# A fused attention and feed-forward kernel: the planner's order replaced by a written one, table loads as tasks of their own, separate banks for the first transposes, one silu for the last chunk

## The chip, the cores and the metric

The kernel runs on one core of a Trainium2 chip. A core has five instruction streams that matter here: PE (TensorE: matmuls and transposes, with the weight loads listed apart as PEld), DVE (VectorE), ACT (ScalarE), POOL (GpSimd) and SP (SyncE, which issues most DMAs). Each stream is carried out in its own order; they wait for one another through semaphores. Matmuls write to PSUM, which has eight banks of 128 partitions by 512 float32 numbers; ACT and DVE empty them.

The metric is the device time of one launch in microseconds (us). The profile is one execution, taken by the hardware profiler; its "span" leaves out what lies around the program.

## The reference

The input `x` has 2048 tokens of 448 numbers. It is normalised once, and the result feeds two branches whose outputs are multiplied:

```python
def _A_ref(x, wqkv, wo):            # H = 16 heads of Dh = 28, W = 8 keys, 2 apart
    qkv = (x @ wqkv).reshape(B, S, 3, H, Dh) ...
    idx = pos[:, None] - (arange(8) * 2)[None, :]
    logits = where(idx >= 0, q . k[idx] * Dh ** -0.5, -1e9)
    o = softmax(logits) . v[idx]
    return o.reshape(B, S, D) @ wo

def _B_ref(x, w1, b1, w2, b2):      # 448 -> 1792 -> 448
    return gelu_tanh(x @ w1 + b1) @ w2 + b2

xn = layernorm(x)
return x + _A_ref(xn, ...) * silu(_B_ref(xn, ...))
```

## The kernel before

**Tiling.** Tokens are split into even and odd ones, so that a dilation of 2 becomes neighbours. There are 16 token tiles of 128 (NT) in four chunks of 512 (NCH). The 448 features are three full row tiles of 128 and one of 64; the last one is held twice, so that two matmuls of 64 rows can run side by side in the array.

**Steps.** For each token tile: `stats` (DVE), `rstds` (ACT and DVE for tiles 0 to 3, POOL for the rest), `norm` (DVE), and a transposition of the normalised tile into `xnT`. Tiles 0 to 3 are transposed by PE into a PSUM bank and copied out by ACT or DVE; the rest go through a DMA transpose on SP. `qk_rows` and `vproj` (lines 532 and 556) make q, k and v; q and k are transposed by DMA into `qkT`, and rows of v are moved by POOL's DMAs into window buffers. For the first two tiles `first_batch` runs three full row tiles of q, k and v together, `kt` = 0, 1, 2, each needing its own third of `w_in`. All other projections and the first feed-forward layer `ff1` (line 591) are made in pairs (`pair`): four row-tile steps, a no-op on SP or POOL that waits for them, then three more steps. Each pair takes two banks, and its two results are emptied by ACT (gelu, line 595) or copied by ACT or DVE. `ff2` (line 627) takes seven gelu results at a time into one bank; then `y` = bank + b2 on DVE, tanh on ACT (line 655), and `g` = (tanh + 1) * y on DVE (line 659).

**Attention** goes in nine blocks. "S" (line 677): 64 small matmuls of 32 rows fill four banks with scores; ACT takes the exponentials (line 687) and DVE or POOL multiply by a mask (line 693). "P" (line 709): 64 matmuls of 64 rows and 32 columns sum the values into two banks; DVE then transposes, inverts, transposes back and multiplies into `oT` (lines 719 to 733). `final` (line 796) multiplies `oT` by `wo`; DVE makes `sg` = bank * 0.5 * g (line 801), `o` = x + sg (line 807), and SP stores it.

**What sets the order.** Every step is a task (`_Task`) with an engine, a cost, dependencies and the buffers that it takes and gives back. `_Plan.run` lets all engines go through the tasks in modelled time and picks by hand-set priorities (`PRIO`, `LATER`); `emit` writes the instructions in the order of the modelled start. An instruction waits only for what it needs, but nothing on its engine overtakes it. ACT needs another function table for square root, for gelu and for exp; a load stands in front of the first activation that needs it, and `tanh` is in the table of either of the latter two. Some 14 to 17 matmuls on a zeroed tile (`warm`, line 327) run at the start.

Of the kernel before, what the change touches and what calls it, by code (L numbers as in the profile page):

```python
# [13 lines left out]
HOP = 0.10  # L14
SLACK = 0.12
TABLE = 1.28
SWITCH = 0.095
TILED = 30
SAME = 20
HOPS = ("POOL", ("SP", "POOL"))  # L20
MASK_ON = (("DVE", "POOL"), (0.4, 1.2))


def VISITS(bs):
    out = [[("S", b)] for b in bs[:2]]
    for i, b in enumerate(bs):
        out.append([("P", b)] + [("S", c) for c in bs[i + 2:i + 3]])
    return out


class _Pool:


    def __init__(self, bufs, fifo=False):
        self.bufs = bufs
        self.fifo = [] if fifo else None
        self.free = [(0.0, i) for i in range(len(bufs))]


class _Task:  # L40
    __slots__ = ("eng", "cost", "deps", "fn", "prio", "take", "give", "slots",
                 "start", "end", "on", "ndep", "users", "tail", "seq", "table", "limit", "mode", "out")


class _Plan:

# [4 lines left out]
    def add(self, eng, cost, fn, deps=(), prio=0, take=(), give=(), tail=0.0, table=(), limit=None,  # L53
            mode=128):
        t = _Task()
        t.eng = eng if isinstance(eng, tuple) else (eng,)
        t.cost = cost if isinstance(cost, tuple) else (cost,) * len(t.eng)
        t.deps = [d for d in deps if d is not None]
        t.fn, t.prio, t.give, t.tail, t.table, t.limit = fn, prio, give, tail, table, limit
        t.mode, t.out = mode, None  # L60
        t.take = {}
        for p in take:
            t.take[p] = t.take.get(p, 0) + 1
        t.slots = {}
        t.start = t.end = None
        t.on = None
        t.users = []
        t.seq = len(self.tasks)
        self.tasks.append(t)
        for p in t.take:  # L70
            if p.fifo is not None:
                p.fifo.append(t)
        return t

    def _at(self, t, e, free):
        at = free.get(e, 0.0)
        for p, n in t.take.items():
            if len(p.free) < n or p.fifo and p.fifo[0] is not t:
                return None
            at = max(at, sorted(p.free)[n - 1][0] + HOP)  # L80
        if t.table and self.table not in t.table:
            at += TABLE
        for d in t.deps:
            at = max(at, d.end - d.tail if d.on == e else d.end + HOP)
        if e == "PE" and t.mode != self.mode:
            at = max(at, free.get(e, 0.0) + SWITCH)
        return at

    def run(self):
        for t in self.tasks:  # L90
            t.ndep = len(t.deps)
            for d in t.deps:
                d.users.append(t)
        free = {}
        self.table = None
        self.mode = 128
        ready = [t for t in self.tasks if not t.ndep]
        order = []
        while ready:
            cand = []  # L100
            for t in ready:
                ways = []
                for e, c in zip(t.eng, t.cost):
                    at = self._at(t, e, free)
                    if at is not None:
                        ways.append((at + (c if len(t.eng) > 1 else 0.0), at, e, c))
                if ways:
                    _, at, e, c = min(ways)
                    cand.append((at, t, e, c))
            if not cand:  # L110
                raise RuntimeError("the plan is stuck: " + str([(t.seq, t.eng, t.fn.__qualname__) for t in ready[:20]]))
            first = min(cand, key=lambda k: k[0])
            near = [k for k in cand if k[2] == first[2] and k[0] <= first[0] + SLACK]
            tiled = first[2] == "PE" and self.mode < 64
            at, t, e, c = min(near, key=lambda k: (-k[1].prio - (TILED if tiled and k[1].mode < 64 else SAME if k[2] == "PE" and k[1].mode == self.mode else 0),
                                                   k[0], k[1].seq))
            if t.limit is not None and at > t.limit:
                t.fn, c = None, 0.0
            t.on, t.start = e, at
            if e == "PE" and t.fn is not None:  # L120
                self.mode = t.out or t.mode
            if t.table and self.table not in t.table:
                self.table = t.table[0]
            free[e] = at + c
            t.end = at + c + t.tail
            for p, n in t.take.items():
                got = sorted(p.free)[:n]
                for g in got:
                    p.free.remove(g)
                t.slots[p] = [g[1] for g in got]  # L130
                if p.fifo is not None:
                    p.fifo.pop(0)
            for p, owner, i in t.give:
                p.free.append((t.end, owner.slots[p][i]))
            ready.remove(t)
            order.append(t)
            for u in t.users:
                u.ndep -= 1
                if not u.ndep:
                    ready.append(u)  # L140
        assert len(order) == len(self.tasks)
        self.order = sorted(order, key=lambda t: (t.start, t.seq))
        self.span = max(t.end for t in order)
        return self

    def emit(self):
        done = set()
        for t in self.order:
            for d in t.deps:
                assert id(d) in done  # L150
            done.add(id(t))
            if t.fn is not None:
                t.fn(t)

# [10 lines left out]
def kernel(  # L165
# [12 lines left out]
    nc = tc.nc  # L178
# [67 lines left out]
    def ring(name, n, shape, dt=BF16, fifo=False):  # L246
        return _Pool([sb(f"{name}{i}", shape, dt) for i in range(n)], fifo)
# [3 lines left out]
    p_E = ring("E", 8, [P, 512], fifo=True)  # L251
# [10 lines left out]
    p_h = ring("h", 28, [P, CH], fifo=True)  # L262
    p_v = ring("v", 6, [P, H, 32], fifo=True)
    qk_tok = [sb(f"qk_tok{i}", [P, 2, H, 32]) for i in range(4)]
    p_b = _Pool([psum.tile([P, 512], F32, name=f"bank{i}") for i in range(8)])

    p_tok = _Pool([None])


    PRIO = {  # L270
        "project": (49.5, 205, 104, 52.5,),
        "project2": (147, 150, 101, 61,),
        "values": (89.5, 62.5, 21, 58,),
        "attn": (185, 179.5, 78, 174.5, 106.5, 106, 138.5, 136.5, 32.5,),
        "ff1": (185, 180, 84.5, 176.5, 66.5, 64.5, 156.5, 189.5, 203, 146, 76, 114.5, 77.5, 179.5,
            75.5, 118.5, 180.5, 14.5, 163, 68, 151, 115.5, 194.5, 167.5, 180, 188.5, 86, 93,),
        "gelu": (62.5, 22.5, 95, 92.5,),
        "ff2": (144, 162.5, 103.5, 142.5, 44.5, 112.5, 67, 5, 89, 106.5, 101.5, 75, 74, 55, 11.5,
            6.5,),
        "final": (140, 19.5, 70.5, 47, 112, 34.5, 23.5, 142.5, 73, 53, 198.5, 188.5, 81.5, 126.5,  # L280
            180, 71,),
        "norm": (37.5, 132, 179.5, 129.5, 74.5, 99, 161, 69, 63, 62, 43.5, 73, -5.5, 90, 133.5,
            150,),
        "loads": (166.5, 166, 188, 139.5, 54.5,),
        "stats": (47.5, -60, 180.5, 23, 127, 56, 188.5, 77, 197.5, -13.5, 185, 205.5, 138, 14, 52.5,
            138.5,),
        "turn_x": (108.5, -1, 28, 116, 210, 116.5, 131.5, 160, 41.5, 79.5, 70, 119, -4.5, 74.5,
            132.5, 111,),
        "turn_qk": (68.5, 112, 174.5, 90, 80, 6, 149.5, 60.5, 4, 140.5, 199.5, 96.5, 103, 166.5,
            140, 156,),  # L290
        "move_v": (81.5, 95, 23, 95, 18.5, 26.5, 8, 128, 29.5,),
        "copies": (50, 119.5, 58.5, 76, 32.5, 135.5, 43, 1, 87, 79.5, 129, 77, 32, 41.5, 135,),
    }
    LATER = {"swap": 135, "qk": 165, "v": 29.5, "gelu": 30.5, "exp": 55.5, "mask": -60, "pv": 45, "recip": -16.5, "os": 54.5, "y": 153.5, "tanh": 182.5, "g": 58, "sg": 183, "o": 120.5}
# [5 lines left out]

    def pe(n, k=1):
        return k * (n / 2400.0 + 0.0025)

    def act(n):
        return 0.15 + n / 1130.0

    def dve(n, r=1):
        return 0.15 + n / (960.0 * r)
# [12 lines left out]

    warm = p_h.bufs[-1]
    t_on = plan.add("DMA", 0.8, lambda _: None, (), 100)
    t_warm = plan.add("DVE", 0.3, memset("vector", warm[:], 0.0), [t_on], prio=100)
    for i in range(48):
        def fn(k, n=512 if i < 9 else P):
            nc.tensor.matmul(buf(p_b, k)[:, :n], warm[:, :P], warm[:, :n], start=True, stop=True)  # L327
# [288 lines left out]
    def ff2_part(t, cs, n, end, prio):  # L616
# [26 lines left out]
        if t == NT - 1:  # L643
            prio += 9
# [322 lines left out]
```

## Time and profile before

| what | value |
|---|---|
| time, median of 3 runs | 157.99 us (157.61 to 159.14) |
| span of the profiled execution | 156.2 us |
| PE busy | 150.1 us |
| matmuls of the second layer (L627, 238) | 45.2 us |
| matmuls of the first layer (L591, 392) | 44.7 us |
| matmuls of q, k (L532, 212) and v (L556, 106) | 24.3 and 13.4 us |
| matmuls of the output (L796, 68) | 14.1 us |
| function table loads on ACT | 6, of 1.28 us each |
| DVE busy between 59 and 94 us | 31.4 of 35 us |

The page gives, for each group of instructions, the busy time, the mean duration, and the idle time of its engine before it with what ended it. Idle time of an engine costs something only if someone waits for that engine. The chain of waits is followed back from the last instruction, so it says what held the end back. A matmul's record is longer than the time that it holds the array up (a 448-column matmul is 0.35 us long, and the next starts 0.19 us after it), so PE's pace is read from starts.

### The profile page before, as it was taken

Reading aid. Unit: us, or ns where it says so; the run is one execution under the profiler, and the core shown is the slowest. Engines: PE = TensorE matmul, PEld = TensorE weight load, DVE = VectorE, ACT = ScalarE, POOL = GpSimd, SP = SyncE. Lnnn points to the kernel's source line nnn. Section 1 sums busy time; section 2 is a strip of 40 time slices with the busy share of each in tenths; the row PEclk is TensorE's granted clock in tenths of the full one; section 3 lists DMA queues with packets and bytes.
Section 4 is the critical chain, followed back from the end, with each engine's and each line's share of the span. In section 5 each row is a group of like instructions: output and inputs, shape, how many; then the busy total and the mean of one; then the engine's idle time right before and its main releaser. Section 6 shows DMA issues by size and latency. Waiting matters only on the chain.

```text
span 156.2 us, 5305 instructions
## 1 busy us (share of the span) xinstructions
PE 150.1 (96%) x2204; PEld 77.8 (50%) x2204; DVE 113.2 (72%) x259; ACT 83.3 (53%) x149; POOL 74.7 (48%) x123
## 2 busy tenths in 40 slices
PE   6999999999999999999999999999999999999980
PEld 2544454444455555455554644455556444545570
DVE  4789551486266758997799895109899996998992
ACT  3245867378889416444634149782496587051220
POOL 7854856000459408839261098389599780000000
PEclk9999999999999999999999999999999999999999
DMA  4999969999749443099039822123300100200211
GB/s 156 329 317 315 167 124 187 237 269 307 141 95 166 64 82 90 10 192 138 4 83 85 131 70 73 38 76 83 105 0 4 34 31 29 63 4 0 68 36 43
DMA packets 33575, 17.36 MB, mean 111 GB/s; under 512 B 25331, under 2 KB 32387, under 8 KB 33552
## 3 DMA queue, kind: packets, MB, share of 16 engines
q1 hardware_dynamic: 31472, 14.03, 41.3%
q0 software_dynamic: 1936, 2.88, 8.5%
q8 instruction: 17, 0.28, 0.8%
q10 hardware_dynamic: 144, 0.11, 0.2%
q14 instruction: 6, 0.05, 0.1%
HBM read 7.06 MB, written 1.84 MB: 57 GB/s over the span
## 4 chain that ended last, share of the span: by engine, by line
PE 80%; DVE 8%; DMA 3%; POOL 2%; issue 2%; ACT 1%; SPq 1%; DVEq 0%; ACTq 0%; POOLq 0%
PE bank L627 23%; PE bank L591 22%; PE bank L532 11%; PE bank L796 7%; PE bank L556 6%; PE bank L677 4%; PE bank L709 4%; PE bank L327 3%; DMA xnT<-xn 3%; POOL v L354 2%; DVE sg L801 2%; DVE o L807 1%; DVE w_in L659 1%; ACT E L687 1%; DVE xn L438 1%
## 5 line engine op out<-in xcount | busy, mean ns | idle before, releaser
L627 PE MATMUL bank<-w,h 128*128 128x448 bf16 (+1 forms) x238 | 45.2, 342 | 0.0
L591 PE MATMUL bank<-xnT,w 64*128 64x512 bf16 x392 | 44.7, 376 | 0.0
L595 ACT ACTIVATE h<-bank,b 128x512 bf16<-128x512 f32 x56 | 34.0, 689 | 12.9 <-PE bank L591 12.8
L354 POOL DMA_DIRECT2D v<-v_tok x52 | 27.6, 538 | 19.8 <-PE bank L709 9.0
L693 POOL TENSOR_TENSOR E<-E,m_gen 128x456 bf16<-128x456 bf16 x24 | 26.7, 1139 | 11.7 <-ACT E L687 9.5
L627 PEld LDWEIGHTS <-h 128*128 128x128 bf16 x238 | 22.3, 98 | 18.1 <-issue 0.4
L591 PEld LDWEIGHTS <-w 64*128 64x128 bf16 x392 | 19.1, 94 | 22.7 <-issue 1.1
L532 PE MATMUL bank<-w_in,xnT 64*128 64x448 bf16 (+1 forms) x212 | 24.3, 350 | 0.1
L687 ACT ACTIVATE E<-bank 128x456 bf16<-128x456 f32 (+1 forms) x36 | 17.0, 555 | 9.1 <-PE bank L677 9.1
L655 ACT ACTIVATE t<-y 128x448 f32<-128x448 f32 x15 | 8.7, 578 | 17.4 <-DVE y L649 17.4
L719 DVE STREAM_TRANSPOSE dt<-bank 128x480 f32<-128x480 f32 (+1 forms) x18 | 12.1, 671 | 5.6 <-PE bank L709 5.6
L532 PEld LDWEIGHTS <-xnT 64*128 64x128 bf16 (+1 forms) x212 | 10.6, 94 | 10.9 <-issue 1.1
L314 DVE CAST qk_tok<-bank 128x448 bf16<-128x448 f32 x16 | 9.4, 613 | 6.8 <-PE bank L532 6.8
L796 PE MATMUL bank<-wo,oT 128*128 128x448 bf16 (+1 forms) x68 | 14.1, 342 | 0.0
L312 ACT CAST qk_tok<-bank 128x448 bf16<-128x448 f32 x16 | 8.3, 533 | 10.6 <-PE bank L532 10.0
L556 PE MATMUL bank<-w_in,xnT 64*128 64x448 bf16 (+1 forms) x106 | 13.4, 349 | 0.0
L649 DVE TENSOR_TENSOR y<-bank,b 128x448 f32<-128x448 f32 x15 | 9.3, 620 | 4.9 <-PE bank L627 4.9
L728 DVE STREAM_TRANSPOSE dt<-rd 128x480 f32<-128x480 f32 (+1 forms) x18 | 12.1, 673 | 0.5
L733 DVE TENSOR_TENSOR oT<-bank,dt 128x456 bf16<-128x456 f32 (+1 forms) x18 | 11.3, 630 | 0.5
L404 DVE BATCH_NORM_STATS2 st<-x_sb 128x6 f32<-128x448 bf16 x16 | 9.6, 603 | 2.4 <-DMA x_sb<-in_A_x_dram 2.4
L438 DVE TENSOR_SCALAR xn<-x_sb,mv,rstd 128x448 bf16<-128x448 bf16 x16 | 6.3, 394 | 6.0 <-POOL rstd L426 5.8
L796 PEld LDWEIGHTS <-oT 128*128 128x128 bf16 x68 | 6.3, 98 | 6.3 <-issue 0.8
(62 smaller groups left out, 128.9 us busy)
## 6 DMA issues: line engine op xcount, KB each, us to landing
out_dram<-o SPq DMA_DIRECT2D x15, 112.0 KB, 1.7
w<-in_B_w_dram SPq DMA_DIRECT2D x2, 784.0 KB, 7.2
w<-in_B_w_dram SPq DMA_DIRECT2D x2, 672.0 KB, 7.0
x_sb<-in_A_x_dram SPq DMA_DIRECT2D x3, 448.0 KB, 6.3
v<-v_tok POOLq DMA_DIRECT2D x20, 64.0 KB, 2.5
w_in<-in_A_wqkv_dram SPq DMA_DIRECT2D x3, 336.0 KB, 4.3
w<-in_B_w_dram SPq DMA_DIRECT2D x4, 112.0 KB, 6.5
wo<-in_A_wo_dram POOLq DMA_DIRECT2D x4, 98.0 KB, 4.2
```

Of the source, the lines that this page charges most:

```text
L354: nc.gpsimd.dma_start(dst(k), src())
L532: return nc.tensor.matmul(ps[:, :D], xnT[r, kt, cs], w, start=start, stop=stop)
L556: return nc.tensor.matmul(ps[:, :D], xnT[r, kt, k0:k0 + P], w, start=start, stop=stop)
L591: return nc.tensor.matmul(ps[:], w1[r, kt, ms], xnT[r, kt, cs], start=start, stop=stop)
L595: nc.scalar.activation(buf(p_h, own, i)[:], buf(p_b, own, i)[:], ACT.Gelu_apprx_tanh, bias=b1[:, mt:mt + 1])
L627: nc.tensor.matmul(ps[:, :n], buf(*h_at[(c, mt)])[:, j * P:(j + 1) * P], w2[:, mt, cs], start=(mt == 0 and not biased), stop=(mt == NMT - 1))
L687: nc.scalar.activation(buf(p_E, k)[:, :n], buf(p_b, a, at + hl)[:, :n], ACT.Exp, scale=SCALE)
L693: (nc.gpsimd if k.on == "POOL" else nc.vector).tensor_tensor(out=E[:, :n], in0=E[:, :n], in1=m[:, :n], op=ALU.mult)
L719: nc.vector.transpose(buf(p_dt, k)[:, :32 * m], buf(p_b, po, i)[:, :32 * m])
L728: nc.vector.transpose(buf(p_dt, d)[:, :32 * m].rearrange("p (b c) -> p b c", c=32), buf(p_rd, r)[:, :m].unsqueeze(2).to_broadcast((P, m, 32)))
L733: nc.vector.tensor_tensor(out=oT[:, :, q0:q0 + 2 * nq], in0=buf(p_b, po, i)[:, :n].rearrange("p (l q) -> p l q", l=4), in1=buf(p_dt, d)[:, ...
L796: nc.tensor.matmul(ps[:, :n], oT[:, kt, t * P:(t + 1) * P], wo[:, kt, cs], start=(kt == 0), stop=(kt == KT - 1))
```

## The change

1. The planner with its costs and priorities goes; the text `ORDER` lists every task by engine (P for PE, V for DVE, A for ACT, G for POOL, S for SP, D for the end of a transfer) and number. Buffers are handed out first come, first served in that order. Tasks may now stand elsewhere than before; dependencies that served only the planner (gates between gelu and exp, and between `ff2` and `final`) go too.
2. `norm`: for tiles 0 and 1 the two halves of the transposition go to banks of their own, with a copy each.
3. `table`: six one-column activations (gelu, exp, gelu, exp, gelu, silu) into a scratch column, as tasks that can be put anywhere on ACT.
4. `ff2_part`, chunk 3: one silu on ACT in place of tanh on ACT and `g` on DVE; `final_part` then multiplies without the 0.5.
5. `final_part`: `o` may run on POOL in all chunks. 17 warming matmuls are always emitted.

```diff
-HOP = 0.10
-SLACK = 0.12
-TABLE = 1.28
...
+ORDER = """
+D0 V1 P2 P3 P4 P5 P6 P7 P8 P9 P10 G54 P11 P12 S38 D39 V19 V26 G55 D56 V30 A40 D41 P13 V33 G35 V20 V64 V65 S44 D45
+A57 A66 V68 V67 G21 G108 S46 D47 V69 V110 G106 A70 V71 S48 D49 S42 D43 V111 V117 V118 S50 D51 P14 P15 P16 S52 D53
+P194 P112 A114 P17 P113 P119 V195 S84 D85 A121 P18 V72 V34 S82 D83 P120 A115 A122 V27 D123 D116 V24 V73 A74 V22 V29
...
+S890 P677 A676 V836 V837 A670 V838 P681 P678 V909 S910 D911
...
+"""
...
-    def run(self):
...
+    def emit(self, order):
+        words = order.split()
+        assert len(words) == len(set(words)) == len(self.tasks)
+        for word in words:
+            t = self.tasks[int(word[1:])]
+            on = self.ENGINES[word[0]]
+            assert on in t.eng and t.on is None and all(d.on for d in t.deps)
+            t.on = on
             for p, n in t.take.items():
+                t.slots[p] = [p.free.pop(0) for _ in range(n)]
             if t.fn is not None:
                 t.fn(t)
+            for p, owner, i in t.give:
+                p.free.append(owner.slots[p][i])
...
+    sink = sb("sink", [P, 1], F32)
+    def table(func):
+        plan.add("ACT", lambda _: nc.scalar.activation(sink[:], eps_t[:], func), [t_eps])
+    table(ACT.Gelu_apprx_tanh)
+    table(ACT.Exp)
+    table(ACT.Gelu_apprx_tanh)
+    table(ACT.Exp)
+    table(ACT.Gelu_apprx_tanh)
+    table(ACT.Silu)
...
+        halves, apart = [], t < 2
         for i in range(2):
             def f3(k, i=i):
-                xn, tp = buf(p_xn, a), half_bank(buf(p_b, (halves or [k])[0]))
+                xn, tp = buf(p_xn, a), half_bank(buf(p_b, k if apart else (halves or [k])[0]))
...
+        if c == NCH - 1:
+            def silu(k):
+                nc.scalar.activation(buf(p_g, k)[:, :n], buf(pool, y)[:, :n], ACT.Silu)
+            t_g[t].append(plan.add("ACT", silu, after, take=(p_g,), give=held))
+            return
...
         def f2(k):
+            if t >= NT - TPC:
+                nc.vector.tensor_tensor(out=buf(p_sg, k)[:, :n], in0=buf(p_b, a)[:, :n], in1=buf(p_g, g)[:, :n], op=ALU.mult)
+                return
...
-        o = plan.add(("DVE", "POOL") if t < 2 * TPC else "DVE", ...
+        o = plan.add(("DVE", "POOL"), f3, [s], take=(p_o,), give=((p_sg, s, 0),))
```

What stands where in the new order, as far as the steps below use it (read from the order of the two built programs): SP's first loads were x tile 0, `w_in` kt 0, `w_in` kt 2, x tiles 2 and 3, `w_in` kt 1; they are now x tile 0, x tiles 2 and 3, `w_in` kt 1, kt 2, kt 0 (S38, S44, S46, S48, S42). The bias row b1 is loaded first on POOL and transposed on PE before the first tile (P194) instead of after the first projections. The two programs have the same 2,204 matmuls. ACT has eight table loads instead of six: the exp table before the second half of attention is loaded by a scratch activation (A61), the silu table by another (A63) ahead of the last chunk's gelus, so that gelu's is loaded again after it, and silu's again at the end; the other three scratch activations stand where their table is loaded already.

## The prediction

> **What bounds the kernel now.** I read the busy times first, then the chain of waits, then the timeline of PE, and at the places where PE is not what is followed, the engines around it. The busy times and the chain by engine:
>
> ```profile
> PE 150.1 (96%) x2204; PEld 77.8 (50%) x2204; DVE 113.2 (72%) x259; ACT 83.3 (53%) x149; POOL 74.7 (48%) x123
> ...
> PE 80%; DVE 8%; DMA 3%; POOL 2%; issue 2%; ACT 1%; SPq 1%; DVEq 0%; ACTq 0%; POOLq 0%
> ```
>
> Busy PE is not proof, so I check its pace. The chain of waits in order of time has long pieces of it:
>
> ```profile
> 23.10 4.16 DMA xnT<-xn
> 27.27 0.04 issue
> 27.31 2.07 PE bank L532 x20
> 29.38 12.95 PE bank L591 x120
> ...
> 119.40 1.43 PE bank L627 x7
> ...
> 141.80 1.32 PE bank L627 x7
> ```
>
> 120 first-layer matmuls, two at a time, take 12.95 us, 0.216 per couple; seven of the second layer take 1.32, 0.189 each; a visit to the scores or the values takes 0.61. Summing all matmuls from 6.61 us (the first projection) to PE's last at 151.5 with these prices leaves about 5 us, and most of that is one kind of thing: the first group after a change between full, 64-row and 32-row tiles is 0.08 to 0.11 longer (1.43 against 1.32). So PE has no slack between 6.61 and 151.5; only its start, its few gaps and the end can be gained. The same matmuls are in both kernels.
>
> **The start costs time.** The rows of PE around its first work:
>
> ```profile
> 5.59 0.63 PE L453 MATMUL bank<-ident,xn 128*128 128x128 bf16 x4
> 6.02 0.53 PE L327 MATMUL bank<-h 128*128 128x128 bf16 x3
> 6.61 0.55 PE L532 MATMUL bank<-w_in,xnT 128*128 128x448 bf16 x2
> ```
>
> The first projection needs kt 0 of `w_in`. Before, it was SP's second load. The transfers issued between 1.2 and 1.5 us:
>
> ```profile
> w_in<-in_A_wqkv_dram SPq DMA_DIRECT2D x1, 336.0 KB, 3.0
> ```
>
> So it landed at 1.25 + 3.0 = 4.25, long before 6.61. Asked for 2.6 to 2.9 us, the view gives the load in SP's fifth place, kt 1, with all but the same bytes ahead of it as kt 0 has in the new order:
>
> ```profile
> w_in<-in_A_wqkv_dram SPq DMA_DIRECT2D x1, 336.0 KB, 5.3
> ```
>
> That is 2.66 + 5.3 = 7.96. Loads on this queue landed in the order of issue (x tiles 2 and 3, issued at 2.18, after 4.4; the third place, issued at 1.69, after 4.3, so at 6.0). In the new order the fifth place is what PE needs first: its first projection starts at 8.0 instead of 6.61, **+1.4**. Ends: if it landed as the third place did, nothing; if as the load after it, 3.2 + 5.3 = 8.5, +1.9. I take the fifth place, the same slot and the same bytes.
>
> In the gap PE does what stood inside the batch: four transposes of tile 1 (8 in all, 0.055 each: 0.2), and the batch's waits for its single transposition bank (6.61 to 10.64 is 4.03, for 18 matmuls and 8 transposes that add up to 3.84) mostly go: **-0.4**. The separate banks earn no more than this, since the weights are late. Tile 1 is normalised earlier (in the old order DVE first waited 0.76 for PE), and nobody needs it. The b1 transposition on PE waits for a transfer that was issued at 1.82 and took 4.0; issued first on POOL, at some 1.3, it lands near 5.3, and PE comes to it at 5.9. If that fails, the wait lies under the one for the weights.
>
> **In the middle.** Counting changes of tile shape along PE in both orders gives 43 and 37; six at 0.08 is **-0.5**. The wait for the transposed tiles at 27.27 cost 0.4 (23.50 to 29.21 is 5.7 for 56 matmuls, two at a time, that cost 5.3). In the new order first-layer work stands between these projections and POOL's square roots come ahead of its v rows: **-0.3**, between 0 and -0.4. The other stall is the exp table:
>
> ```profile
> 111.52 1.28 ACT L687 ACT_TABLE_LOAD   x1 [5.00 <-PE bank L677]
> ...
> 114.76 0.65 PE L677 MATMUL bank<-qkT 32*64 32x57 bf16 x58 [0.22 <-ACT E L687]
> ```
>
> The load took on the wait for the scores and ran behind them, so the next visit's four banks came late: 114.14 to 118.09 is 3.95 us for work that costs 3.4. The scratch activation before it waits only for ACT, whose gelus are over by then: **-0.5**. The other loads ahead save nothing: at 15.41 ACT waited for b1, at 46.24 and 94.69 it was loading while PE worked on.
>
> Moving masks between DVE and POOL (POOL 24 to 21, DVE 12 to 15), five `g` fewer and seven `o` on POOL takes some 4 us off DVE, of 113; in 59 to 94 us DVE was busy for 31.4 of 35 and PE stood still nowhere, so that is worth nothing in itself. What DVE does cost is order. Behind the visit to the values at 105 us of the old trace, it now has, before the `y` that frees a bank for the last scores: eight stream transposes (0.67), four reciprocals (0.25), four multiplications into `oT` (0.63), two `sg` and two `y` (0.62), three masks (0.39) and a `g` (0.62, 1.23 where POOL is busy): 13.2 to 13.8, less about 0.08 of overlap at half of the steps: 12.4 to 13.1. Then a tanh (0.58) and one exponential (0.55) free the last bank: 13.5 to 14.2, while PE has 13.8 of work until it needs it. The chain goes on through seven more DVE steps to the bank of the following first-layer pair: 17 to 18 against PE's 16.7. So a loss of 0 to 1.6; **+0.8**, the middle, since rows of both lengths stand in that stretch.
>
> Also at this place: silu's table, loaded ahead of the last gelus, and gelu's loaded again, two more loads of 1.28 and a 0.2 activation. PE's next five pairs have eight banks, and the first one is wanted again some 2 us after the gelus can begin, so I cost it at nothing; without that cover it is 1.5. The Trainium skill (ScalarE: Activation LUTs, What ACT_TABLE_LOAD costs) puts a switch at 2.66 us with a drain. Here a load of 1.28 is followed by its activation 0.01 later (46.24, 47.53), so the row decides; by the page the sum would be about 1 us more.
>
> **The end.** The last rows of PE and DVE:
>
> ```profile
> 150.75 0.93 PE L796 MATMUL bank<-wo,oT 128*128 128x224 bf16 x8
> ...
> 152.19 0.38 DVE L659 SCALAR_TENSOR_TENSOR w_in<-t,bank 128x224 bf16<-128x224 f32 x1
> 152.68 0.39 DVE L801 SCALAR_TENSOR_TENSOR sg<-bank,w_in 128x224 bf16<-128x224 f32 x1
> 153.10 0.28 DVE L807 TENSOR_TENSOR o<-x_sb,sg 128x224 bf16<-128x224 bf16 x1
> ```
>
> PE issues its last work until 151.5, and DVE's last `o` ends at 153.38, 1.9 later, because DVE is behind since 144.7. Chunk 3 now has no `g`: four of 0.62 and two of 0.38 go, with the dependent tanh. What is left behind PE is its latency (0.2), `sg` and `o` of one half (0.42 + 0.28) and a little of the other's: 1.0. **-0.85**. The store's 2.8 us behind it stays.
>
> **Sum.** 1.4 - 0.4 - 0.5 - 0.3 - 0.5 + 0.8 - 0.85 = -0.35. The profiled execution's span is 156.2, 1.8 under the median of 157.99; so a span of 155.8 and a time of 157.6.
>
> **The rivals.** *The first weights are not late*, as other columns of the queue's load finish faster than I read them: the +1.4 falls away, 156.2. For it: kt 0 before took just 3.0. Against: three landings in order of place.
>
> *A transfer stuck behind POOL's no-op* (the other side). The no-op of a pair (G653) makes POOL wait for PE; behind it stand a mask (1.14) and the last v rows (G500) for the values visit P830. PE has 4.4 us of work between (two half pairs, 12 output matmuls, one visit). POOL needs 0.1 + 1.14 and the landing. In the old trace v rows landed in 1.6 to 3.5 at 100 to 112 us, and in 4.1 to 5.2 at 48 to 51. Up to 3.1 nothing is late; at 5.2 PE stands for 2.1: 159.7. It ends slower than before from 3.6 on. Against it: this stretch's queues are light.
>
> *The array's clock falls back* while PE is idle from about 6.5 to 8.0. The first 14 matmuls took 4.55 us, 0.43 per 512 columns, twice the later pace. If PE had to go through as long a slow time again, 4.4 us at half pace, it would cost 2.2: 159.8. Against it: no other gap here is long enough to show it. The Trainium skill (TensorE: Matmul & The Clock Gate, Part 1) has the clock halve only after an idle window of some 3.4 us; by that rule, this does not happen.
>
> *The loads ahead do the contrary*: the silu load costs its 1.5, so 159.1.
>
> **How the numbers follow.** Forecast 0.58, with 156.5 to 158.6 of its own (the stretch of DVE 0 to 1.6, the transposed tiles 0 to 0.4, the weights by some tenths); weights in time 0.15; POOL 0.14; clock 0.07; table 0.06. The range reaches down to the weights' case and up to most of POOL's: 156.0 to 159.4. A measurement of this kernel tells about 1% from no change, 156.4 and 159.6: faster 0.19 (over half of the weights' case and the low end of the forecast), slower 0.14 (POOL's and the clock's upper ends, the highest of the rest), same 0.67.
>
> **What would show it.** In the new profile the first L455 matmul should start at 7.9 to 8.1, released by the transfer of `w_in`; at 6.7 the first step is wrong. Matmuls after it at 0.19 mean that the clock held. No exp load should have a wait for scores ahead of it near 110 us. PE's gaps should lie between 112 and 126 us, released by DVE or ACT; a gap ahead of the last values visit released by a v row is POOL's case. DVE's last `o` should end 1.0 after PE. A time outside of the range would mean that the orders in the middle, which I took as equally dense, are not.

## The result, and the profile after

The changed kernel takes 165.07 us (median of 4 runs, 164.47 to 165.76), the kernel before 158.01 in the same series: 1.044 times as long (95% interval 1.039 to 1.049). The forecast was 157.6, and the range ended at 159.4. The profiled execution has a span of 162.6 us, 1.9 under its own time of 164.47, as before; so the span is 6.4 longer.

The page after: the busy times, the granted clock in 40 slices of 4.07 us, and the chain of waits by engine.

```profile
PE 151.5 (93%) x2204; PEld 79.3 (49%) x2204; DVE 110.2 (68%) x246; ACT 89.0 (55%) x165; POOL 74.1 (46%) x123
...
PEclk9969999999999999999999999999999999999999
...
PE 68%; DVE 20%; DMA 4%; ACT 2%; issue 2%; SPq 1%; DVEq 0%; ACTq 0%
```

DVE has less work than before (110.2 against 113.2), and yet it holds 20% of the chain instead of 8. The clock has a slice of 0.6 where it had none. What PE waited for over the whole span (total, times, longest) names the places. The three dots stand for PE's first wait, of 1.2 us, which the kernel before has too:

```profile
PE bank L455 <- DMA w_in<-in_A_wqkv_dram: 2.7, 1, 2.7
PE bank L547 <- DVE sg L690: 1.5, 1, 1.5
PE bank L628 <- DVE qk_tok L231: 1.3, 1, 1.3
...
PE bank L682 <- DVE oT L652: 0.6, 1, 0.6
```

**The start.** PE in order of time:

```profile
6.37 0.28 PE L379 MATMUL bank<-ident,xn 128*128 128x128 bf16 x2
9.34 0.83 PE L455 MATMUL bank<-w_in,xnT 128*128 128x448 bf16 x2 [2.69 <-DMA w_in<-in_A_wqkv_dram]
9.97 0.58 PE L478 MATMUL bank<-w_in,xnT 128*128 128x448 bf16 x1
10.34 0.95 PE L455 MATMUL bank<-w_in,xnT 128*128 128x448 bf16 x2
...
13.10 0.35 PE L478 MATMUL bank<-w_in,xnT 128*128 128x448 bf16 x1
13.29 0.54 PE L455 MATMUL bank<-w_in,xnT 128*128 128x448 bf16 x2
```

The first projection starts at 9.34 instead of 6.61: kt 0 was issued at 2.71 and landed 6.59 us later. Behind it, from 9.34 to 10.34 there are three matmuls where 0.57 us would do, and the next ones go at 0.37 each and not at 0.19. That is the granted clock: 0.50 over 3.4 us, from 9.45 to 12.85, and 1.00 on either side. The first eleven matmuls take 3.76 us (9.34 to 13.10); at 0.19 each they would take 2.09, so 1.67 us is lost.

**The middle.** DVE and POOL ahead of the wait of 1.3 us (PE's second matmul of the values visit stands from 71.6 to 72.88 for a bank that the first of the last two copies here frees):

```profile
68.17 2.06 POOL L612 TENSOR_TENSOR E<-E,m_gen 128x456 bf16<-128x456 bf16 x2
...
69.08 1.86 DVE L369 COPY xn<-xn 128x64 bf16<-128x64 bf16 x1
70.17 0.67 POOL L264 DMA_DIRECT2D wo<-in_A_wo_dram  x1
...
70.85 1.20 DVE L364 TENSOR_SCALAR xn<-x_sb,mv,rstd 128x448 bf16<-128x448 bf16 x1
70.86 1.06 POOL L612 TENSOR_TENSOR E<-E,m_gen 128x456 bf16<-128x456 bf16 x1
72.09 0.18 DVE L369 COPY xn<-xn 128x64 bf16<-128x64 bf16 x1
72.20 1.16 DVE L231 CAST qk_tok<-bank 128x448 bf16<-128x448 f32 x2
```

The same copy of 64 columns takes 1.86 us in one place and 0.18 in the other. The long one begins while POOL makes masks and ends at 70.94, 0.1 after the DMA issue that POOL does right behind them. The normalisation takes 1.20 while POOL makes a mask. Over the kernel, by form (count, busy us, mean ns):

```profile
L364 DVE TENSOR_SCALAR xn<-x_sb,mv,rstd 128x448 bf16<-128x448 bf16 x16 | 10.0, 629 | 8.1 <-POOL rstd L352 8.1
...
L612 DVE TENSOR_TENSOR E<-E,m_gen 128x456 bf16<-128x456 bf16 x13 | 8.3, 656 | 0.0
...
L369 DVE COPY xn<-xn 128x64 bf16<-128x64 bf16 x16 | 5.1, 326 | 0.3
```

Before, the means were 394, 388 and 183 ns. The difference, times the counts, is 3.8 + 3.5 + 2.3 = 9.6 us more in which DVE is listed as busy and, as the runs below show, stands still. So "DVE 110.2" hides a loss: the count fell, the durations rose.

**The account.** Against before: first projection 2.7 later, pace behind it 1.67, waits at 72.9 and 82.4 us 2.0, waits at 125 and 127.4 us 1.7; from the end of PE's last matmul (159.31, before 151.68) to DVE's last `o` (160.12, before 153.38) 0.81 instead of 1.70, so -0.9; the last store 0.3 shorter. That is 6.8 of 6.4; the rest of the order gave back 0.4.

### The profile page after: what moved, and what is told of

It reads as the page before. It is cut to its first block, busy times and chain, and to the rows that moved or that the text cites. A ratio compares the mean times of both kernels' runs of the same rounds, so it can differ in the third digit from the quotient of the medians.

```text
span 162.6 us, 5267 instructions
## 1 busy us (share of the span) xinstructions
PE 151.5 (93%) x2204; PEld 79.3 (49%) x2204; DVE 110.2 (68%) x246; ACT 89.0 (55%) x165; POOL 74.1 (46%) x123
## 4 chain that ended last, share of the span: by engine, by line
PE 68%; DVE 20%; DMA 4%; ACT 2%; issue 2%; SPq 1%; DVEq 0%; ACTq 0%
PE bank L513 25%; PE bank L547 15%; PE bank L455 11%; PE bank L478 7%; PE bank L682 6%; DMA w_in<-in_A_wqkv_dram 4%; DVE E L612 3%; PE bank L628 2%; DVE oT L652 2%; DVE y L562 2%; DVE dt L647 2%; DVE g L578 2%; DVE dt L638 2%; PE bank L596 2%; DVE sg L690 1%
## 5 line engine op out<-in xcount | busy, mean ns | idle before, releaser
L517 ACT ACTIVATE h<-bank,b 128x512 bf16<-128x512 f32 x56 | 34.9, 690 | 11.7 <-PE bank L513 11.6
L271 POOL DMA_DIRECT2D v<-v_tok x52 | 28.2, 548 | 22.6 <-PE bank L513 9.5
L513 PEld LDWEIGHTS <-w 64*128 64x128 bf16 x392 | 19.7, 94 | 22.3 <-issue 1.0
L455 PE MATMUL bank<-w_in,xnT 64*128 64x448 bf16 (+1 forms) x212 | 25.7, 356 | 2.7 <-DMA w_in<-in_A_wqkv_dram 2.7
L612 POOL TENSOR_TENSOR E<-E,m_gen 128x456 bf16<-128x456 bf16 x15 | 16.4, 1097 | 11.3 <-PE bank L513 6.0
L696 POOL TENSOR_TENSOR o<-x_sb,sg 128x448 bf16<-128x448 bf16 x7 | 7.5, 1078 | 21.8 <-DVE sg L690 9.8
L364 DVE TENSOR_SCALAR xn<-x_sb,mv,rstd 128x448 bf16<-128x448 bf16 x16 | 10.0, 629 | 8.1 <-POOL rstd L352 8.1
L229 ACT CAST qk_tok<-bank 128x448 bf16<-128x448 f32 x23 | 11.5, 538 | 6.8 <-PE bank L455 4.2
L478 PE MATMUL bank<-w_in,xnT 64*128 64x448 bf16 (+1 forms) x106 | 13.9, 356 | 0.0
L574 ACT ACTIVATE t<-y 128x448 f32<-128x448 f32 x12 | 6.6, 578 | 12.7 <-DVE y L562 12.7
L231 DVE CAST qk_tok<-bank 128x448 bf16<-128x448 f32 x9 | 5.4, 619 | 7.1 <-PE bank L455 4.1
```

The costliest lines, as they stand in the source:

```text
L271: nc.gpsimd.dma_start(dst(k), src())
L455: return nc.tensor.matmul(ps[:, :D], xnT[r, kt, cs], w, start=start, stop=stop)
L478: return nc.tensor.matmul(ps[:, :D], xnT[r, kt, k0:k0 + P], w, start=start, stop=stop)
L513: return nc.tensor.matmul(ps[:], w1[r, kt, ms], xnT[r, kt, cs], start=start, stop=stop)
L517: nc.scalar.activation(buf(p_h, own, i)[:], buf(p_b, own, i)[:], ACT.Gelu_apprx_tanh, bias=b1[:, mt:mt + 1])
L612: (nc.gpsimd if k.on == "POOL" else nc.vector).tensor_tensor(out=E[:, :n], in0=E[:, :n], in1=m[:, :n], op=ALU.mult)
```

## The experiments

Each was timed beside the kernel before, whose medians were 157.9 to 158.2. In the experiments' kernels most line numbers are one lower than in the changed kernel.

### The start: load order, and the idle time alone

SP's first loads in the old order:

```diff
 S38 D39
+S42 D43 S48 D49
...
 S44 D45
...
 S46 D47
...
-S48 D49 S42 D43
```

> The changed kernel with SP's first loads in the old order (x tile 0, kt 0, kt 2, x tiles 2 and 3, kt 1). Theory A, the start costs the wait for kt 0 (2.7 us) and a slow clock behind it (nine full-row matmuls at 0.37 instead of 0.19, 1.65): 4.3 us less, a median of 160.7, first projection at 6.6 to 6.7 and 0.19 per matmul from there. Theory B, only the wait counts and the pace of the first nine matmuls has another cause: 2.7 less, 162.4. Theory C, the late start is hidden by the stretches in which DVE is behind later: under 1.5 less.

161.1 us (160.77 to 161.44), 4.0 less: theory A. The first projection starts at 6.82 and goes at 0.19. PE's waits of 1.5, 1.3 and 0.6 us for DVE are all still there, so the late start had hidden nothing of them.

With kt 0 still late, work for PE in the gap:

```diff
+    for i in range(10):
+        def fn(_):
+            nc.tensor.matmul(p_b.bufs[p_b.free[0]][:], warm[:, :P], warm[:], start=True, stop=True)
+        extra.append(plan.add("PE", fn, [t_warm]))
```

> The changed kernel, kt 0 still late, with ten more matmuls of 512 columns on the zeroed tile between the first transposes and the first projection, so that PE idles 0.5 us there and not 2.7. If the idle time lets the clock fall (theory A): the first nine full-row projections at 0.19, 1.6 us less, a median of 163.4. If the slow pace has another cause (theory B): 165.1, or a little more should the added matmuls outlast the wait.

163.15 us (162.47 to 163.76), 1.9 less: theory A again. PE in this run:

```profile
6.47 2.32 PE L806 MATMUL bank<-h 128*128 128x512 bf16 x10
9.59 0.54 PE L455 MATMUL bank<-w_in,xnT 128*128 128x448 bf16 x2 [0.79 <-DMA w_in<-in_A_wqkv_dram]
9.97 0.35 PE L478 MATMUL bank<-w_in,xnT 128*128 128x448 bf16 x1
10.15 0.54 PE L455 MATMUL bank<-w_in,xnT 128*128 128x448 bf16 x2
```

The projection even starts 0.25 later than in the changed kernel, and its three matmuls take 0.56 instead of 1.0. Useless work that keeps the array busy is worth 1.9 us: here the idle time is what slows the clock.

The same load order in the kernel before, all else kept:

```diff
+    first = [t_x[2], t_w[1][0], t_w[2][0], t_w[0][0]]
...
+        if i in at:
+            new += pairs[k]
...
+    plan.order = new
```

> The kernel before, its order kept, with SP's first loads in the order of the changed kernel (x tile 0, x tiles 2 and 3, kt 1, kt 2, kt 0). By the prediction's step: kt 0 lands at 8.0, 1.4 us later start, 159.4. By the trace of the changed kernel: it lands at 9.2 and the clock falls, 2.7 + 1.7 more, 162.4; where the clock holds, 160.7.

161.86 us (161.35 to 162.97; ratio 1.023, 1.019 to 1.028), so 3.8 more. In its trace PE waits 3.35 us and starts at 9.32, the next matmuls 0.37 apart; the granted clock is 0.50 from 7.75 to 14.56. The start alone costs the old kernel what it cost the new one.

### DVE standing still behind POOL

Three masks of 68 to 72 us from POOL to DVE:

```diff
-G715 ... G739 ... G733
+V715 ... V739 ... V733
```

> The changed kernel with three masks that POOL makes between 68 and 72 us (G715, G739, G733) on DVE, in the same places of the order. Theory D, DVE's normalisation steps stand still while POOL works (a 64-column copy of 1.86 us instead of 0.18, a normalisation of 1.20 instead of 0.39): these are short again, DVE comes 1.3 us sooner to the qk_tok copy in spite of three masks of 0.39 more, the wait of the values visit at 71.4 (1.3 us) goes: a median of 163.8. Theory E, DVE has simply too many steps ahead of that copy: two more of 0.39 make the wait 2.1 and the median 165.8.

163.36 us (161.16 to 164.27), and the wait of 1.3 us is no longer in the list. DVE in the same place:

```profile
67.53 0.17 DVE L368 COPY xn<-xn 128x64 bf16<-128x64 bf16 x1
67.61 0.39 DVE L363 TENSOR_SCALAR xn<-x_sb,mv,rstd 128x448 bf16<-128x448 bf16 x1
68.03 0.18 DVE L368 COPY xn<-xn 128x64 bf16<-128x64 bf16 x1
68.13 0.39 DVE L611 TENSOR_TENSOR E<-E,m_gen 128x456 bf16<-128x456 bf16 x1
```

More steps on DVE, and it is done sooner: theory D, against E. (The clock at the start did not fall in the profiled execution, 161.16, though PE idled 2.6 us there too; in the other three it did, by their mean clocks of 0.977 to 0.986. So the median mixes two things. At like clocks, 0.977 and 0.978, two executions took 164.2 and 164.27 us, and the changed kernel at 0.979 took 165.76: 1.5 less, near the 1.3 of the wait.)

Two masks and an `o` of 119 to 124 us in the same way:

```diff
-G805 ... G884 ... G829
+V805 ... V884 ... V829
```

> The changed kernel with two masks and one o that POOL makes between 119 and 124 us (G805, G829, G884) on DVE, in the same places of the order. Theory D (DVE stands still while POOL works): two masks that took 2.9 us together take 0.8, the wait of 1.5 us ahead of the second-layer group at 125 goes in spite of 1.1 us of added steps: a median of 163.6 to 164.1. Theory E (too many steps): 1.1 more, 166.2.

163.86 us (163.31 to 164.14), 1.2 less; the wait of 1.5 us is gone. In the changed kernel one mask of DVE takes 2.40 us, while POOL goes without a pause through a v DMA, an `o` and two more v DMAs:

```profile
120.28 0.55 POOL L271 DMA_DIRECT2D v<-v_tok  x1
120.51 2.40 DVE L612 TENSOR_TENSOR E<-E,m_gen 128x456 bf16<-128x456 bf16 x1
120.85 1.04 POOL L696 TENSOR_TENSOR o<-x_sb,sg 128x448 bf16<-128x448 bf16 x1
121.82 1.06 POOL L271 DMA_DIRECT2D v<-v_tok  x2
```

Here two masks take 0.63 together. Theory D again. The 1.2 understates it: the slow clock at the start lasts 6.8 us in this trace (0.50 from 8.27 to 15.07), twice as long as in the changed kernel's. At a mean clock of 0.979 three executions took 163.64 to 164.14 us, the changed kernel 165.76.

Is it POOL's arithmetic or its DMA issues that DVE stands still for? In the changed kernel seven issues in a row leave DVE's `o` and two masks at their short durations:

```profile
103.55 3.61 POOL L271 DMA_DIRECT2D v<-v_tok  x7 [0.83 <-DVE rd L642]
105.58 0.33 DVE L696 TENSOR_TENSOR o<-x_sb,sg 128x448 bf16<-128x448 bf16 x1
105.83 0.69 DVE L612 TENSOR_TENSOR E<-E,m_gen 128x456 bf16<-128x456 bf16 x2
```

All 14 traces together have 159 steps of DVE (`m_gen` masks, normalisations, 64-column copies and full `o`) that in their undisturbed duration had DMA issues of POOL beside them and no arithmetic. Of these, 148 kept that duration. The other 11 are one normalisation in 11 kernels: it takes 1.28 us, beginning right behind POOL's `rstd` (52.62 in the changed kernel, `rstd` until 52.58) beside two issues. So an issue as such does not make DVE stand still. Next to POOL's arithmetic it can prolong it, and what decides is open.

All three repairs at once:

> The changed kernel with three of its parts put right at once: the old order of SP's first loads, the three masks of 68 to 72 us and the two masks and the o of 119 to 124 us on DVE. If the three losses add up (4.0, 1.3 and 1.2 us by the runs of one part each): 158.4 us, level with the kernel before. If they overlap, because DVE's backlog of one stretch is carried to the next: 159.5 or more.

157.59 us (157.28 to 158.74, 12 runs; ratio 0.998, 0.996 to 1.000). That is 0.8 better than the 158.4 of the sum, not worse, so none of the three losses hides another. By the values at like clocks, 1.5 and 1.7 instead of 1.3 and 1.2, the sum would be 157.9; the changed kernel's side of these is a single execution. What is left of the change is level with the kernel before or 0.4 better. The other parts were tried on this kernel.

### The end, the table loads

The last chunk's gate by tanh and `g` again:

```diff
-                nc.scalar.activation(buf(p_g, k)[:, :n], buf(pool, y)[:, :n], ACT.Silu)
+                nc.scalar.activation(tb[:, :n], yb[:, :n], ACT.Tanh, scale=0.5)
...
+                    nc.vector.scalar_tensor_tensor(out=gb[:, :n], in0=tb[:, :n], scalar=1.0, in1=yb[:, :n],
+                                                   op0=ALU.add, op1=ALU.mult)
```

> As the run with the three parts put right, but the last chunk's gate by tanh on ACT and g on DVE again, and no silu table loaded anywhere. If the one silu saves what the prediction says: 0.85 us slower, 159.2. If the end is hidden by something else (the two tanhs and g's fit under PE): the same, 158.4.

159.14 us (158.78 to 159.36), 1.55 more: the silu is worth that here. DVE is back in the chain of waits at the end (start, us, engine and line):

```profile
152.47 0.39 DVE o L712
152.86 0.31 DVE w_in L577
...
154.36 0.40 DVE sg L706
...
154.78 0.28 DVE o L712
```

The last `o` ends 2.35 after PE (152.71 to 155.06), with the silu 0.81. The place of each `g` in DVE's order is mine, one step behind its tanh, so a hand-set order might do a little better. The other way round, the silu alone in the kernel before:

```diff
+            if c == NCH - 1:
+                nc.scalar.activation(buf(p_g, gate[0])[:, :n], buf(pool, y)[:, :n], ACT.Silu)
+                return
```

> The kernel before, its order kept, with the last chunk's gate by one silu on ACT and no g on DVE. By the prediction's step on the end: 0.85 us less, 157.2. By the run that undid the silu: 1.5 less, 156.5. If the silu's table load at the end is in the way: no gain.

157.45 us (156.89 to 158.35, 12 runs; ratio 0.996, 0.993 to 0.998): 0.6 less, with 1.04 from PE's end to the last `o` instead of 1.70.

One silu table load, behind the last gelu, instead of two (`A63` moved to stand right before `A680`):

> As the run with the three parts put right, but the silu table is loaded once, after the last gelu, and not also ahead of the last chunk's gelus, so there are two table loads fewer. By the prediction's step (the loads are covered by PE's full banks): the same, within 0.3 us. By its rival (the loads ahead hold up the gelus): up to 1.5 less, 156.9.

157.52 us (157.49 to 157.74), the same. The loads ahead of the gelus cost nothing: in the changed kernel ACT was done with them and still waited 0.31 us for PE's first pair.

A gelu in place of the exp in the scratch activation at 112 us:

```diff
-    table(ACT.Exp)
+    table(ACT.Gelu_apprx_tanh)
```

> As the run with the three parts put right, but the scratch activation that fetches the exp table at 112 us is a gelu, so that the load falls behind the wait for the scores at 117, as in the kernel before. By the prediction's step: 0.5 us slower, 158.9. If the banks are not needed back that early in the new order: the same.

157.59 us (157.39 to 157.81), the same. ACT there:

```profile
110.66 1.28 ACT L605 ACT_TABLE_LOAD   x1 [3.39 <-DVE oT L651]
112.36 1.88 ACT L605 ACTIVATE E<-bank 128x456 bf16<-128x456 f32 x4 [0.42 <-PE bank L595]
```

Left to itself, the load did not go behind the scores: it waited for a step of DVE, ran at 110.66 and was over before the scores came. The load took on one of the waits of its activation, and in this order that is an early one. So this run does not show what a load behind the scores would cost.

### Mending what is left

From here on the silu table is loaded once. An `o` (G864) on DVE, the zeroing of `wo` (G37) behind the first normalisations, and two masks behind a `y`:

```diff
-V863 G864
+V863 V864
...
-V31 G37 V28
+V31 V28
...
+P160 G161 G37
...
-V898 A844 V845 V825 P638 G823 V639
+V898 A844 P638 G823 V639 V845 V825
```

> As the run with the three parts put right and the silu table loaded once, with three more places mended: the o of 73 us (G864) on DVE, so that the mask behind it does not stand still; the zeroing of wo on POOL (G37) behind the first normalisations; two masks (V845, V825) behind the y that frees a bank at 124 us. If DVE standing still behind POOL is what is left of the losses: 0.6 for the wait of 77 us, 0.2 to 0.4 at the start, up to 0.5 at 124 us, so 156.0 to 156.7. If the chain of DVE's steps sets the pace of these stretches whatever their lengths: the same as that run, 157.5.

159.11 us (157.71 to 160.03, 12 runs), 1.6 more: a miss. The transposes of tile 2 came 0.5 us sooner (9.79 against 10.28) and DVE left the chain at 124 us, but at 73 us the collision moved on: POOL, now without that `o`, makes a mask from 73.22, and DVE's `o` and `g` take 0.57 and 1.47. PE then waits 0.20 and 0.90, and in the profiled execution the clock falls. PE by stretches (busy us and count, granted clock, DMA share, GB/s):

```profile
76.00:78.00 2.00, 1.10 (x61) 1.00 0.03 8
78.00:80.00 2.00, 2.00 (x14) 0.60 0.00 0
80.00:82.00 2.00, 2.00 (x16) 0.54 0.00 0
82.00:84.00 2.00, 2.00 (x24) 1.00 0.37 98
```

The 50 projections on 64-row tiles from 78.19 on take 6.43 us to the next group, 4.74 in the run with one silu load. By their mean clocks the fall came in seven of the 12 executions (0.986 to 0.989, 159.0 to 160.0 us). The other five (0.998 and above) took 157.7 to 158.75, so even with a full clock nothing was gained.

The `o` back on POOL, the other two edits kept, and DVE's order changed so that the mask starts before POOL does:

```diff
-V531 P567 P568 V737 A756 V579 V728 V729 V730
+P567 P568 V737 A756 V728 V729 V730 V531 V579
```

> As the run before with more places mended, but the o of 73 us stays on POOL; instead a mask (V737) and the three steps to oT (V728 to V730) stand ahead of the g and the y (V531, V579) on DVE, so that the mask starts before POOL does. If the last three waits go (0.65 at 77 us, 0.2 to 0.4 at the start, up to 0.5 at 124 us) and PE's clock holds, since PE no longer waits behind the two visits of small tiles: 156.0 to 156.4, under both kernels. If the collision moves on to another step once more: 157.5 or above.

156.6 us (155.89 to 157.58; ratio 0.992, 0.989 to 0.995), faster than both kernels, and a little above the expectation:

```profile
73.92 0.39 DVE L611 TENSOR_TENSOR E<-E,m_gen 128x456 bf16<-128x456 bf16 x1
74.09 1.10 POOL L695 TENSOR_TENSOR o<-x_sb,sg 128x448 bf16<-128x448 bf16 x1 [8.44 <-DVE sg L689]
```

The mask starts 0.17 ahead of POOL's `o` and takes 0.39; in the run with one silu load it took 1.22. The wait of 77 us is gone from PE's list, and DVE's steps of 105 to 125 us from the chain of waits. The edit did two things for that wait: the short mask, and the steps to `oT` ahead of `g` and `y`; how much each did was not tried. One longer wait is left: in this trace kt 1, the fifth load, comes 0.98 us late.

## Why the prediction was wrong, step by step

The forecast had the span 0.35 us shorter; it is 6.4 longer. The start accounts for 3.0 of the difference (weights 1.3 more than forecast, clock 1.67), DVE's waits for 2.9 (2.0 where the sum had nothing, 0.9 more than forecast at 125 us), gains that fell short for 1.3; the last store gave back 0.3. The prediction took a time outside its range as a sign of orders less dense in the middle: that is the second item, not the first.

- **"+1.4", the late weights: mis-sized, 2.7 us.** The mechanism was the right one, released by the transfer as it said. But kt 0 was used from 9.13 to 9.59 in the five traces with x tiles 2 and 3 in second place, the kernel before with the new load order among them, and not at 8.0. The 5.3 us of the fifth place was one load of one trace, taken as if a queue's place and bytes fixed the landing. In the eight traces with the old load order for which the view has it, the fifth place took 5.3, 5.6, 5.9, 5.9, 6.1, 6.5, 6.6 and 6.7 us. The row was the shortest of them, and the longest lands at 9.4. What sets this is not settled: between 3.6 and 5.0 us the transfers moved 179 GB/s in the changed kernel and 299 before, but 247 in the trace where kt 0 came latest.
- **The clock falling back, a rival with 0.07: it happened**, in every timed run of the changed kernel by its mean clock (0.979 to 0.990). The price of 2.2 was 1.67 in the trace and 1.9 by the run that filled the gap. I gave it little because no gap of the old trace was long enough to show it, and leaned on a rule. The Trainium skill (TensorE: Matmul & The Clock Gate, Part 1) has the clock fall after an idle window of some 3.4 us. Here 2.69 us was enough, so the measurement decides against it as a bound.
- **"-0.4", the batch's waits and transposes.** Not tried alone. The transposes of tile 1 did move ahead of the batch. The batch took 5.40 us (9.34 to 14.74) with four transposes in it; less the 1.67 that is 3.73, against 4.03 with eight, so about 0.3 came.
- **"Worth nothing in itself" for moving masks and `o` between POOL and DVE: the step that failed.** I counted DVE's steps by their undisturbed durations and asked whether PE stood still in the old order. The old trace had the sign (a `g` of 1.23 "where POOL is busy"), and I used it for one step of one stretch. It holds for masks, normalisations and copies too, and so an engine with less work fell behind. PE stood still for 1.3 and 0.65 us between 59 and 83 us, where I had nothing at all; the run with three masks on DVE shows it for the first of the two waits. The Trainium skill (SBUF — State Buffer, Who interferes with whom) has it: such DVE instructions and GpSimd share a port pair, held for a whole instruction by whoever comes first. The traces agree (0.39 when DVE starts 0.17 first, 1.22 when POOL does). They add that 0.01 ahead by the records is not enough (the normalisation at 70.85, POOL's mask at 70.86), and that DVE's mask of 2.40 us stood on through two DMA issues behind POOL's `o`. The count was wrong too: masks went from 28 to 21 on POOL and from 8 to 15 on DVE (I had put four of POOL's on DVE), and seven q and k copies, which I had not counted, went from DVE to ACT.
- **"+0.8", DVE's order behind 105 us: right place, mis-sized.** 1.5 + 0.2 us, with two masks of 2.9 together that the sum had at 0.8. (Its allowance for overlap, 0.08 at half of 24 steps, is 0.96 and not 0.7 to 0.8; that alone would have made the term smaller.)
- **"-0.5", the exp table: no gain from the scratch activation in this order.** The old stall at 111 us is gone, but without the scratch activation it stays gone.
- **"-0.5" and "-0.3", shape changes and transposed tiles.** The chain runs on PE without a break from 9.34 to 60.07, so nobody waits for the transposed tiles any more. With the batch and the exp table they were to give 1.7; the account leaves 0.4 for all of it, net of waits too short for the list. Which of them fell short was not tried.
- **The loads ahead at no cost: right** (0.1 us of difference). POOL's no-op rival did not come: no wait ahead of the last values visits.
- **"-0.85" at the end: right in the trace** (1.70 to 0.81); as a change of time 0.6 in the old kernel, 1.55 in the new. Of the long `g`, three went and not four (DVE's `g` of 448 columns: 15 before, 12 after).

That the three repairs bring the time to 157.6, the very number of the forecast, is chance: that kernel has no late start, which the sum had at 1.4.

## What to carry to other kernels

Where one engine can stand still behind another, as DVE behind POOL here, count for each step the time at which the other one works, not only the steps: look in a by-form list for one shape with two durations. Take the landing of a load from several traces, not from one. Before a first load is moved back, look at what the consumer does until then: an idle tensor engine of 2.7 us cost 2.7 and 1.67 more here, and matmuls on zeros in the gap saved the second part. An order by hand lives by its few worst waits, so list those of the new trace first and mend them one at a time.

## What the runs showed of the hardware

- The clock fell after 2.69 and 3.35 us of an idle PE, and in one kernel with 2.6 us in some executions and not in others. Where a trace has the fall at the start, the granted clock is 0.50 for 3.4 us (9.45 to 12.85 in the changed kernel) or for twice as long (8.27 to 15.07 with the masks and `o` of 119 us on DVE). Why 2.6 us is sometimes enough was not settled.
- It also fell in the middle of a kernel (0.60, then 0.54, between 78 and 82 us) behind two visits of small tiles and waits of 0.20 and 0.90 us; with one wait of 0.65 at the same place it did not. The runs do not part the waits from the small tiles.
- POOL's zeroing of `wo` holds up DVE like its masks: in the run with one silu load a normalisation takes 1.25 us beside it (8.97 to 10.22, POOL until 10.09) and not 0.39. With nothing of POOL beside them but DMA issues, 148 of 159 steps of DVE kept their duration.
- The fifth load on SP's queue, the same bytes in the same order, took between 5.3 and 6.7 us from issue to landing.
- A table load went out with one of the waits of its activation: at 110.66 ahead of the scores in one run, behind them in the old order.
